# Half of a block's attention by seven half-width products, and the first block's additions ahead of an MLP block's low part

## The chip, the cores and the metric

The kernel runs on one core of one Trainium2 chip. The metric is the device time of one execution in microseconds (us); lower is better. Engines are named as in the profile: PE is TensorE's matmuls, PEld its weight loads, DVE is VectorE, ACT is ScalarE, POOL is GpSimd, SP issues DMAs.

## The reference

`x` is 2048 tokens of 512 features. It is normalised, and an attention branch and an MLP branch are added to it.

```python
def _A_ref(x, wqkv, wo):                      # 32 heads of 16
    q, k, v = split_heads(x @ wqkv)
    phi = lambda t: jnp.where(t > 0, t + 1, jnp.exp(t)) + 1e-6
    pq, pk = phi(q), phi(k)
    kv = jnp.einsum("bhsd,bhse->bhde", pk, v)
    z = jnp.einsum("bhsd->bhd", pk)
    num = jnp.einsum("bhqd,bhde->bhqe", pq, kv)
    den = jnp.einsum("bhqd,bhd->bhq", pq, z)[..., None] + 1e-6
    return join_heads(num / den) @ wo

def _B_ref(x, w1, b1, w2, b2):                # 512 -> 1376 -> 512
    h = jnp.einsum("bsd,df->bsf", x, w1) + b1
    r = jnp.where(h > zero, h, zero)
    return jnp.einsum("bsf,fd->bsd", r * r, w2) + b2

xn = _layernorm(x, axis=-1)
out = x + _A_ref(xn, A_wqkv, A_wo) + _B_ref(xn, B_w1, B_b1, B_w2, B_b2)
```

## The kernel before

The 2048 tokens are 16 tiles of 128, and four tiles are a block of 512 tokens. Every fp32 operand is split into a high part (ScalarE's copy, in a rounded format) and a low part (VectorE's difference, `rest_of` or the second half of `split`), and a product is three matmuls: high by high, high by low, low by high (`PASSES`).

The first stage normalises the tiles and sums keys times tokens. From that one 512 by 512 matrix `m` is made that holds the attention's values and `wo` together, so that the attention's output for a tile is its scaled queries (`aT`) times `m`: four feature chunks of three matmuls, twelve products of 512 columns (`add_attention`).

The second stage runs over two pairs of blocks, `n` = 0 and 1. In a pair, the first-layer products for the two blocks `t1` and `t2` go through a scheme with seven instead of eight products (`product`, in the PSUM banks `b0` to `b3`, tag "ps"). The MLP has 11 feature blocks of 128, the last a ragged one. Its second layer (`mlp_2`, twelve products of 512 columns for four tiles) accumulates in four banks `acc` of the tag "acc"; after `t1` is done, `t2` accumulates in the four banks of the tag "ps" and the roles of the tags change. `wait_for(f)` squares and splits the hidden values of feature block f for `t2`; `waiting` lists these blocks in the order 9, 8, ..., 0, 10. `quarters_2` adds the ragged block's remaining low part by four matmuls of 32 rows each, packed side by side in the array; for `t2` they are the first to write its accumulators.

In the second pair, `t1`'s attention is made by the class `Seven`, also with seven products instead of eight: the block's tokens are halves (rows r), the features are halves (columns c), VectorE makes four sums of `q` in place (`sums_o`) and four of `m` (`sums_m`), both are split into parts (`parts_o`, `parts_m`), and `run` makes one product for one tile of a half as six matmuls of 256 columns. `("a", ...)` names an original quarter of the queries, `("s", ...)` a summed one, `("m", ...)` and `("t", ...)` the same of the matrix. Some products belong to several parts of the result. They go to banks x and y and VectorE adds them from there to the result tiles `res`, which hold `x` and the bias; after that the accumulators are added and each tile is stored. The second block of the pair, `t2`, gets its attention by `add_attention` for all four tiles, after nine of its eleven MLP blocks; the last two MLP blocks (0 and 10) follow tile by tile, with the last tile in two halves (`end`).

The order of instructions on each engine is that of the code. It is written out by hand, partly in tables of counts (`AT`, `AE`) that say how many of the pending small steps (`steps`: phi, the quotients, the splits of `aT`) come at each place. Tiles of one tag rotate through their buffers; an instruction that writes a reused buffer waits for the last reader.

Of the kernel before, what the change touches and what calls it, by code (L numbers as in the profile page):

```python
# [10 lines left out]
OP = mybir.AluOpType  # L11
AX = mybir.AxisListType

P = 128
# [4 lines left out]
def kernel(  # L19
# [30 lines left out]
    nc = tc.nc  # L50
    xf = x.rearrange("b s d -> (b s) d")
    of = out.rearrange("b s d -> (b s) d")
    S, D = xf.shape
    F = w1.shape[1]
    NT = S // P
    NJ = D // P
    TB = 4
    NB = NT // TB
    BT = TB * P
    NF = -(-F // P)  # L60
# [20 lines left out]
    def bank(name, tag="ps"):  # L81
        return psum.tile([P, 512], F32, name=name, tag=tag)
# [54 lines left out]
    def both(name, tags, dt=F32R, pool=keep):  # L137
        return [pool.tile([P, NJ, D], dt, name=f"{name}{u}", tag=t) for u, t in zip("hl", tags)]
# [263 lines left out]
    q = {}  # L402
# [114 lines left out]
    def add_attention(acc, i, last=False):  # L517
        b, k = i // TB, i % TB
        for j in range(NJ):
            a = [aT[b, j][:, u, k * P:(k + 1) * P] for u in range(2)]  # L520
            three(acc[k], a, [m[u][:, j, :] for u in range(2)], False, last and j == NJ - 1)
# [7 lines left out]
    t, rk = two("x0"), four("rk", "r0")  # L529
# [7 lines left out]
    t = two("x2")  # L537
# [17 lines left out]
    for i0 in range(0, NT, TB):  # L555
        a = first_xp[i0]
# [4 lines left out]
        n = TB if i0 >= NPE else TB // 2  # L561
# [36 lines left out]
    for k in range(2):  # L598
        a = slice(k * D // 2, (k + 1) * D // 2)
# [153 lines left out]
    def do(what, k=1):  # L753
        for _ in range(k):
            if what:
                what.pop(0)()
# [57 lines left out]
    for i in range(2, NT):  # L814
# [13 lines left out]
        ps = pks[i] if i < 3 else bank(f"pk{i}")  # L828
# [28 lines left out]
        if i == 12:  # L857
            w = load_1("q", 0)
# [3 lines left out]
        if i == 14:  # L862
            z = pair("w1z0")
# [62 lines left out]
    m = both("m", ("mh", "ml"), pool=work)  # L926
# [43 lines left out]
    LO, HI = slice(0, D // 2), slice(D // 2, D)  # L970

    class Seven:

        def __init__(self, t, acc):
            self.t, self.acc = t, acc
            self.o = [[q[t][:, 2 * c:2 * c + 2, r] for c in range(2)] for r in (LO, HI)]

        def sums_o(self):

# [27 lines left out]

        def parts_o(self):

            self.s = both("so", ("xs1h", "xs1l"))  # L1010
            return self.parts(q[self.t], self.s, ((1, LO), (0, LO), (0, HI), (1, HI)))

        def parts_m(self):

# [2 lines left out]
        def run(self, ps, left, right, e, first=False):  # L1017

            c, r = left[1:]
            for i in range(2):  # L1020
                for n, (u, v) in enumerate(PASSES):
# [4 lines left out]
                    nc.tensor.matmul(ps, lhsT=a, rhs=b, start=first and i == 0 and n == 0, stop=False,  # L1026
                                     skip_group_check=True)


    last = TB - 1  # L1030
    for n in range(2):
        t1, t2 = NB - 1 - 2 * n, NB - 2 - 2 * n
        x1, x2 = xsb
# [24 lines left out]
        steps = {t1: [], t2: []}  # L1058
        r2 = [work.tile([P, k, 512], F32, name=f"r2{u}{n}", tag=f"r{u}") for u, k in zip("abc", (4, 4, 3))]
        waiting = [*range(NF - 2, -1, -1), NF - 1]  # L1060
# [32 lines left out]
        w = load_1(*order[1])  # L1093
        s = {}
# [23 lines left out]


        banks = [bank(f"b{n}_{k}") for k in range(4)]  # L1120
        t5, res, biased = None, {}, []

        def load_res(t):
            for k in range(2):
# [17 lines left out]
        def add(ps, t, k, a=0, z=D):  # L1142
            r = res[t, k]
            nc.vector.tensor_tensor(out=r[:, a:z], in0=ps, in1=r[:, a:z], op=OP.add)  # L1144
# [5 lines left out]
        def step(k=1):  # L1150

            for _ in range(k):
                do(steps[t1] or steps[t2])
# [6 lines left out]
        for p in range(NO + 1):  # L1160
            at_p = AT[p]
            kind, k = order[p] if p < NO else ("", 0)
            fa, fb = 2 * k, 2 * k + 1

            was, k = order[p - 1] if p else ("", 0)
# [27 lines left out]
            if kind:  # L1193
                c11 = w512(f"c11_{n}_{p}", "p", 6)
                copy("act", c11, A)
                product(B, A12, [x[:, 2:] for x in x1], True, True)
                if kind == "w":
                    high_2()
                nc.vector.tensor_tensor(out=c11 if kind == "w" else q[t1][:, fa], in0=B, in1=c11, op=OP.add)
                if kind == "w":  # L1200
                    relu(c11, c11, fa)
                else:
                    steps[t1] += steps_of(t1, fa, parts=True)
                if (n, p) == (0, 0):
                    last_sums(3, difference_high, difference_low)
                if n and p == NO - 1:
                    seven = Seven(t1, acc)
                    sums = seven.sums_o()
                    do(sums, 3)
                step(at_p[0])  # L1210
# [26 lines left out]
            t5 = t5_  # L1237
# [4 lines left out]
            if p == 1:  # L1242
                nc.vector.tensor_scalar(zc[:, 1], zc[:, 0], 1e-6, None, op0=OP.mult)
                acc = [bank(f"acc{t1}_{k}", "acc") for k in range(TB)]
# [92 lines left out]
        def wait_for(f):  # L1337
            name = f"s{n}_{t2}_{f}"
            if f < NF - 1:
                s[f] = hidden_2(name, r2[f])  # L1340
            else:
                s[f], rests = hidden_last(name, r2[f])
                rests()
# [16 lines left out]
        f = NF - 2  # L1360
# [12 lines left out]
        for g in waiting[4:9]:  # L1373
            w2next.extend(piece_2(g, place(g)))
        if n:
            y0, x0, x1_, y1 = (bank(f"seven{k}")[:, LO] for k in range(4))
            xs_, ys_ = (x0, x1_), (y0, y1)
            for e in range(2):
                seven.run(xs_[e], ("a", 0, 0), ("m", 0, LO), e, True)
            for e in range(2):  # L1380
                add(xs_[e], t1, e, 0, D // 2)
            for e in range(2):
                seven.run(acc[e][:, LO], ("a", 1, 0), ("m", 1, LO), e)
            for e in range(2):
                seven.run(acc[e][:, HI], ("s", 1, 0), ("m", 1, HI), e)
            do(lows_m, 4)
            for k in range(TB):
                three(acc[k], [s1[:, u, k * P:(k + 1) * P] for u in range(2)], w2s[f], False, False)
            wait_for(waiting[0])
            for e in range(2):  # L1390
                seven.run(xs_[e], ("s", 0, 0), ("t", 1, HI), e)
            for e in range(2):
                add(xs_[e], t1, 2 + e, 0, D // 2)
            wait_for(waiting[1])
            lqs.append(square_last())
            for e in range(2):
                seven.run(ys_[e], ("s", 0, 1), ("t", 0, HI), e, True)
            for e in range(2):
                seven.run(xs_[e], ("s", 1, 1), ("t", 0, LO), e)
            for e in range(2):  # L1400
                r = res[t1, 2 + e].rearrange("p (a z) -> p a z", a=2)
                nc.vector.tensor_tensor(out=r, in0=ys_[e][:, None, :].to_broadcast([P, 2, D // 2]), in1=r, op=OP.add)
            for e in range(2):
                for k in (e, 2 + e):
                    r = res[t1, k]
                    nc.vector.tensor_tensor(out=r[:, HI], in0=xs_[e], in1=r[:, HI], op=OP.add)
            for e in range(2):
                seven.run(acc[2 + e][:, LO], ("a", 1, 1), ("t", 1, LO), e)
        else:
            add_attention(acc, t1 * TB)  # L1410
            wait_for(waiting[0])
            for k in range(1, TB):
                add_attention(acc, t1 * TB + k)
                if k == 2:
                    wait_for(waiting[1])
                if k == 2:
                    lqs.append(square_last())
# [17 lines left out]
        for e, f in enumerate(waiting[:-2]):  # L1435
            mlp_2(acc, f, s.pop(f))
            if e + 3 < NF - 2:
                wait_for(waiting[e + 3])
            if e:
                do(w2next, 2)  # L1440
                if e + 8 < NF:
                    g = waiting[e + 8]
                    w2next.extend(piece_2(g, place(g)))
            if e == 2:
                load_res(t2)
            if e == 4:
                bias = add_bias()
            if e in ((5, 6) if n else (7, 8)):
                do(bias)
            do(prepare, (1, 0, 0, 1, 0, 2, 2, 3, 1, 3, 1)[e])  # L1450
            if n == 0:
                if e == 3:
                    rawz = raw_1(NF - 1)
                if e == 4:
                    z = pair("w1z1")
                    w = load_1("q", 0)
                if e == 6:
                    columns_high(x2, f2)
                if e == 7:
                    split(z[:, 0], z[:, 1], rawz, "act", "dve")  # L1460
                    columns_high(x1, f1)
            step(AE[e])
            if e and 0 < len(parts_2) and len(steps[t2]) <= 5 * (len(parts_2) - 1):
                do(parts_2)
        do(prepare, len(prepare))
        step(len(steps[t2]))
        do(parts_2, NJ)
        for k in range(TB):
            add_attention(acc, t2 * TB + k, n == 1 and k == last)
            if n == 1 and k < 2:  # L1470
                wait_for(last_two[1 - k])
            if n == 0:
                if k == 0:
                    columns_low(x2, f2)
                    for f in reversed(last_two):
                        wait_for(f)
                    columns_low(x1, f1)
                    prepare = operands_first(1, w)
                if k in (0, 2):
                    do(prepare, 2 if k == 0 else 3)  # L1480
# [43 lines left out]
```

## Time and profile before

| | |
|---|---|
| median of 3 runs | 409.03 us (408.76 to 409.52) |
| the profiled execution | 409.1 us, span 407.4 us |
| TensorE matmul, weight loads busy | 401.8 us (99%), 332.3 us (82%) |
| VectorE, ScalarE busy | 321.4 us (79%), 272.7 us (67%) |
| granted TensorE clock | 1.0 |

The span is what the profiler recorded from the first to the last instruction; the execution's own time has 1.7 us more around it. Matmuls overlap in the rows: a row's duration holds the latency of its last product, so the pace is read from start to start. The stretch that matters lies at the end: `t1`'s attention and last MLP block from 349 to 362 us, `t2`'s MLP blocks from 363.5 to 388 us, its attention from 388 to 399 us, the last two MLP blocks to 404 us, and the last store to 407.4 us.

### The profile page before, as it was taken

What the parts mean: (1) busy time and instruction counts of PE and PEld (TensorE: products, weight loads), DVE (VectorE), ACT (ScalarE), POOL (GpSimd) and SP (SyncE); (2) the same over time, 40 slices, a digit from 0 to 9 for tenths busy, and PEclk for the clock granted to TensorE, in tenths of its full rate; (3) what the DMA queues carried; (4) which work ended last, traced back from release to release, by engine and by line L of the source; (5) the groups of instructions that cost most, each with busy time, mean ns of one, the idle gap of its engine ahead of it and who ended that gap; (6) DMA issues with size and microseconds to landing.
All of it is one profiled execution on the core that took longest, in us unless ns stands there. A gap on an engine that the chain in (4) does not pass through costs nothing.

```text
span 407.4 us, 5755 instructions
## 1 busy us (share of the span) xinstructions
PE 401.8 (99%) x1975; PEld 332.3 (82%) x1975; DVE 321.4 (79%) x585; ACT 272.7 (67%) x474; POOL 49.8 (12%) x81
## 2 busy tenths in 40 slices
PE   8999999999999999999999999999999999999996
PEld 7788888888788888888878888888888888888885
DVE  5886666587898989988349997667989688999833
ACT  5677677556788788886818752667687858947430
POOL 5443333220000000030000300000000200000300
PEclk9999999999999999999999999999999999999999
DMA  6857656910553231381564913321121765025712
GB/s 214 275 169 227 202 165 197 257 27 0 136 177 80 77 103 27 109 200 28 208 232 139 199 25 107 112 53 51 51 80 43 217 116 219 2 79 181 103 26 103
DMA packets 47550, 51.10 MB, mean 125 GB/s; under 512 B 8417, under 2 KB 31201, under 8 KB 47138
## 3 DMA queue, kind: packets, MB, share of 16 engines
q1 hardware_dynamic: 45138, 46.55, 37.2%
q0 software_dynamic: 2304, 4.20, 6.7%
q8 instruction: 15, 0.25, 0.2%
q14 instruction: 13, 0.11, 0.1%
q10 hardware_dynamic: 80, 0.00, 0.0%
HBM read 38.81 MB, written 10.75 MB: 122 GB/s over the span
## 4 chain that ended last, share of the span: by engine, by line
PE 97%; DMA 1%; ACT 0%; SPq 0%; DVE 0%; issue 0%
PE acc L133 35%; PE b L497 33%; PE pk L378 11%; PE kx L398 11%; PE acc L508 2%; PE seven L1026 1%; PE pz L133 1%; DMA rk<-in_A_wqkv_dram 1%; PE acc L1026 1%; PE b L133 1%; PE pz0b L133 1%; PE acc L515 0%; PE pkv L937 0%; PE pm L954 0%; PE pt L310 0%; SPq L161 0%
## 5 line engine op out<-in xcount | busy, mean ns | idle before, releaser
L133 PE MATMUL acc<-w2r,s 128*128 128x512 f32 x477 | 113.1, 390 | 0.0
L133 PEld LDWEIGHTS acc<-w2r,s 128*128 128x128 f32 x477 | 89.3, 188 | 19.1 <-issue 0.6
L497 PE MATMUL b<-T,aop 128*128 128x512 f32 x336 | 83.5, 389 | 0.0
L497 PEld LDWEIGHTS b<-T,aop 128*128 128x128 f32 x336 | 63.0, 188 | 13.9 <-ACT t L114 0.8
L1136 POOL DMA_DIRECT2D res<-in_B_b_dram x16 | 14.4, 1083 | 277.3 <-DMA res<-in_A_x_dram 91.5
L398 PE MATMUL kx<-pk,tok 128*128 128x512 f32 x192 | 46.1, 389 | 0.0
L398 PEld LDWEIGHTS kx<-pk,tok 128*128 128x128 f32 x192 | 36.0, 188 | 7.7 <-ACT pk L114 0.2
L497 PE MATMUL b<-xs0h,aop 128*128 128x512 f32 x112 | 36.9, 390 | 0.0
L114 ACT ACTIVATE aop<-S 128x512 fp32r<-128x512 f32 x28 | 17.5, 625 | 12.6 <-DVE S L735 12.6
L133 PE MATMUL acc<-mh,aTsr 128*128 128x512 f32 x80 | 25.6, 389 | 0.0
L359 POOL TENSOR_TENSOR tok<-xp,tok 128x512 fp32r<-128x512 f32 x15 | 20.2, 1346 | 39.8 <-ACT tok L114 39.8
L497 PEld LDWEIGHTS b<-xs0h,aop 128*128 128x128 f32 x112 | 21.0, 188 | 4.4
L125 DVE TENSOR_TENSOR w2r<-r,w2r 128x512 fp32r<-128x512 f32 (+2 forms) x35 | 23.8, 682 | 0.5 <-ACT w2r L114 0.4
L114 ACT ACTIVATE w2r<-r 128x512 fp32r<-128x512 f32 x32 | 19.7, 621 | 6.7 <-PE acc L133 6.0
L122 DVE TENSOR_TENSOR aop<-S,aop 128x512 fp32r<-128x512 f32 x28 | 19.3, 689 | 4.8 <-ACT aop L114 4.4
L497 PE MATMUL b<-xs0l,aop 128*128 128x512 f32 x56 | 21.8, 389 | 0.0
L1144 DVE TENSOR_TENSOR res<-acc,res 128x512 f32<-128x512 f32 x16 | 10.5, 688 | 14.0 <-PE acc L133 12.7
L122 DVE TENSOR_TENSOR s<-c,s 128x512 fp32r<-128x512 f32 x20 | 13.6, 689 | 8.7 <-ACT s L114 8.6
L497 PE MATMUL b<-xs1h,aop 128*128 128x512 f32 x56 | 19.5, 389 | 0.0
L114 ACT ACTIVATE T<-Tf 128x512 fp32r<-128x512 f32 x16 | 9.5, 625 | 14.4 <-DVE Tf L678 14.3
L114 ACT ACTIVATE c<-b 128x512 f32<-128x512 f32 x28 | 16.4, 587 | 2.5 <-PE b L497 2.4
L133 PEld LDWEIGHTS acc<-mh,aTsr 128*128 128x128 f32 x80 | 15.0, 188 | 3.1
(228 smaller groups left out, 804.7 us busy)
## 6 DMA issues: line engine op xcount, KB each, us to landing
r<-in_B_w_dram SPq DMA_DIRECT2D x49, 256.0 KB, 3.4
res<-in_A_x_dram SPq DMA_DIRECT2D x8, 512.0 KB, 4.7
res<-in_B_b_dram POOLq DMA_DIRECT2D x16, 256.0 KB, 5.9
out_dram<-res SPq DMA_DIRECT2D x15, 256.0 KB, 2.2
via<-xp SPq DMA_DIRECT2D x5, 512.0 KB, 2.6
xg<-via SPq DMA_DIRECT2D x20, 128.0 KB, 2.8
xTd<-t SPq DMA_DIRECT2D x8, 256.0 KB, 3.4
x<-in_A_x_dram SPq DMA_DIRECT2D x4, 512.0 KB, 4.2
```

Of the source, the lines that this page charges most:

```text
L114: nc.scalar.activation(o, i, AF.Copy, bias=bias)
L122: ENG[el].tensor_tensor(out=l, in0=src, in1=f32(h), op=OP.subtract)
L125: nc.vector.tensor_tensor(out=l, in0=src, in1=f32(h), op=OP.subtract)
L133: nc.tensor.matmul(ps, lhsT=a[u], rhs=b[v], start=first and n == 0, stop=last and n == 2)
L359: ENG[el].tensor_tensor(out=l, in0=src, in1=f32(h), op=OP.subtract)
L378: nc.tensor.matmul(ps, lhsT=cols(i)[u][:, j, slot(i)], rhs=w[v][:, j, :], start=first and n == 0, stop=last and n == len(steps) - 1)
L398: nc.tensor.matmul(kxp[c], lhsT=tok[i][:, u, c * P:(c + 1) * P], rhs=pk[i][:, v], start=i == 0 and (u, v) == first, stop=i == NT - 1 and ( ...
L497: nc.tensor.matmul(ps, lhsT=a[u][:, j * P:(j + 1) * P], rhs=b[v][:, j, :], start=first and j == 0 and n == 0, stop=last and j == 1 and n == 2,
L508: nc.tensor.matmul(ps, lhsT=s[u][:, k * P:(k + 1) * P], rhs=w2s[NF - 1][u][:, a:z], start=first and u == 0, stop=stop and u == 1)
L1026: nc.tensor.matmul(ps, lhsT=a, rhs=b, start=first and i == 0 and n == 0, stop=False, skip_group_check=True)
L1136: nc.gpsimd.dma_start(r[:, i], b2[None, :].partition_broadcast(P), accum_op=OP.add)
L1144: nc.vector.tensor_tensor(out=r[:, a:z], in0=ps, in1=r[:, a:z], op=OP.add)
```

## The change

Two things change, both in the second pair.

`Seven` takes a list of tiles of each half, and for `t2` a second object, `half`, covers the first tile of each half: tiles 0 and 2. Its attention is made by seven runs of six 256-column matmuls; tiles 1 and 3 keep `add_attention`. Its sums and parts are made during `t2`'s MLP blocks on 128-token quarters (2 x 128 elements a partition). The matrix's sums are those of `t1`. Two banks, `xh` and `yh`, are taken from the tag "acc".

In `t1`, `wait_for(waiting[1])` (feature block 8) moves from before `square_last` to behind the additions from x and y, and the four banks are taken in the order y0, x0, y1, x1 instead of y0, x0, x1, y1.

```diff
     class Seven:
-        def __init__(self, t, acc):
-            self.t, self.acc = t, acc
-            self.o = [[q[t][:, 2 * c:2 * c + 2, r] for c in range(2)] for r in (LO, HI)]
+        def __init__(self, t, pairs=range(2)):
+            self.t = t
+            self.at = [slice(r * BT // 2 + pairs[0] * P, r * BT // 2 + (pairs[-1] + 1) * P) for r in range(2)]
+            self.o = [[q[t][:, 2 * c:2 * c + 2, at] for c in range(2)] for at in self.at]
...
+        def into(self, ps, k, a):
+            r = res[self.t, k][:, a]
+            if a != LO and a != HI:
+                r, ps = r.rearrange("p (a z) -> p a z", a=2), ps[:, None, :].to_broadcast([P, 2, D // 2])
+            nc.vector.tensor_tensor(out=r, in0=ps, in1=r, op=OP.add)
...
         if n:
-            y0, x0, x1_, y1 = (bank(f"seven{k}")[:, LO] for k in range(4))
-            xs_, ys_ = (x0, x1_), (y0, y1)
+            ys_, xs_ = zip(*((bank(f"y{e}")[:, LO], bank(f"x{e}")[:, LO]) for e in range(2)))
...
-            wait_for(waiting[1])
             lqs.append(square_last())
             for e in range(2):
                 seven.run(ys_[e], ("s", 0, 1), ("t", 0, HI), e, True)
             for e in range(2):
                 seven.run(xs_[e], ("s", 1, 1), ("t", 0, LO), e)
...
             for e in range(2):
                 seven.run(acc[2 + e][:, LO], ("a", 1, 1), ("t", 1, LO), e)
+            wait_for(waiting[1])
...
         for e, f in enumerate(waiting[:-2]):
             mlp_2(acc, f, s.pop(f))
             if e + 3 < NF - 2:
                 wait_for(waiting[e + 3])
+            if n and e == NF - 5:
+                do(highs_o, 4)
+                do(lows_o, 4)
...
             step(AE[e])
+            if n and e == NF - 6:
+                step(len(steps[t2]))
+                half = Seven(t2, (0,))
+                half.mt = seven.mt
+                sums = half.sums_o()
+                highs_o, lows_o = half.parts_o()
...
+            if n and e == NF - 6:
+                do(parts_2, NJ)
+                do(sums, 4)
...
-        for k in range(TB):
-            add_attention(acc, t2 * TB + k, n == 1 and k == last)
-            if n == 1 and k < 2:
-                wait_for(last_two[1 - k])
+        if n:
+            xh, yh = (bank(f"{w}h", "acc")[:, LO] for w in "xy")
+            half.run(xh, ("a", 0, 0), ("m", 0, LO), 0, True)
+            half.run(acc[0][:, LO], ("a", 1, 0), ("m", 1, LO), 0)
+            half.run(acc[2][:, LO], ("a", 1, 1), ("t", 1, LO), 0)
+            half.into(xh, 0, LO)
+            for f in reversed(last_two):
+                wait_for(f)
+            add_attention(acc, t2 * TB + 1)
+            add_attention(acc, t2 * TB + last, True)
+            half.run(acc[0][:, HI], ("s", 1, 0), ("m", 1, HI), 0)
+            half.run(xh, ("s", 0, 0), ("t", 1, HI), 0)
+            half.run(yh, ("s", 0, 1), ("t", 0, HI), 0, True)
+            half.into(xh, 2, LO)
+            half.run(xh, ("s", 1, 1), ("t", 0, LO), 0)
+            half.into(yh, 2, ALL)
+            for k in (0, 2):
+                half.into(xh, k, HI)
+        for k in range(TB) if n == 0 else ():
+            add_attention(acc, t2 * TB + k)
```

Below, the runs of `half` are called by their operands: a00, a10, a11, s10, s00, s01, s11.

The first place is VectorE in `t1`, from the low part of feature block 8 (`s_0_8`) to the last addition from the banks (`seven_3357` is x1, `seven_3355` and `seven_3358` are y0 and y1). Before:

```order
L122 TENSOR_TENSOR s_0_8_3432<-r2a_2493,s_0_8_3432 128x512
L125 TENSOR_TENSOR s1q<-r2c_2495,hq_3436 32x128 x4
L1402 TENSOR_TENSOR res_1_3051<-seven_3355,res_1_3051 128x512
L1402 TENSOR_TENSOR res_1_3051<-seven_3358,res_1_3051 128x512
L1406 TENSOR_TENSOR res_0_3049<-seven_3356,res_0_3049 128x256
L1406 TENSOR_TENSOR res_1_3051<-seven_3356,res_1_3051 128x256
L1406 TENSOR_TENSOR res_0_3049<-seven_3357,res_0_3049 128x256
L1406 TENSOR_TENSOR res_1_3051<-seven_3357,res_1_3051 128x256
```

Now (line numbers here are the changed kernel's; L1036 is `into`):

```order
L125 TENSOR_TENSOR s1q<-r2c_2495,hq_3432 32x128 x4
L1036 TENSOR_TENSOR res_1_3051<-y_3355,res_1_3051 128x512
L1036 TENSOR_TENSOR res_1_3051<-y_3357,res_1_3051 128x512
L1036 TENSOR_TENSOR res_0_3049<-x_3356,res_0_3049 128x256
L1036 TENSOR_TENSOR res_1_3051<-x_3356,res_1_3051 128x256
L1036 TENSOR_TENSOR res_0_3049<-x_3358,res_0_3049 128x256
L1036 TENSOR_TENSOR res_1_3051<-x_3358,res_1_3051 128x256
L122 TENSOR_TENSOR s_0_8_3482<-r2a_2493,s_0_8_3482 128x512
```

The low part of block 8 has moved from the front of these eight to their end; everything else keeps its order.

The second place is VectorE at the end of `t2`, from the last split of `aT` on (`so0h`, `so0l` are the parts of `half`'s sums, `w2r` the last two pieces of w2, `s_0_10` and `s_0_0` the last two MLP blocks). Before:

```order
L122 TENSOR_TENSOR aTsr_3498<-q_2510,aTsr_3498 128x512
L125 TENSOR_TENSOR w2r_1020<-r_0_3554,w2r_1020 128x512
L125 TENSOR_TENSOR w2r_1020<-r_10_3581,w2r_1020 64x512
L125 TENSOR_TENSOR w2r_1020<-r_10_3581,w2r_1020 32x512
L125 TENSOR_TENSOR s_0_10_3731<-r2c_2495,s_0_10_3731 64x512
L122 TENSOR_TENSOR s_0_0_3748<-r2c_2495,s_0_0_3748 128x512
L1144 TENSOR_TENSOR res_1_3587<-acc_3_3488,res_1_3587 128x512
L1144 TENSOR_TENSOR res_0_3585<-acc_0_3485,res_0_3585 128x512
```

Now, up to the same two low parts, and then the additions:

```order
L986 TENSOR_TENSOR q_2510<-q_2510 128x2x128 x4
L125 TENSOR_TENSOR so0l<-q_2510,so0h 128x2x128 x4
L125 TENSOR_TENSOR w2r_1020<-r_0_3554,w2r_1020 128x512
L125 TENSOR_TENSOR w2r_1020<-r_10_3581,w2r_1020 64x512
L125 TENSOR_TENSOR w2r_1020<-r_10_3581,w2r_1020 32x512
L1036 TENSOR_TENSOR res_0_3585<-xh,res_0_3585 128x256
L125 TENSOR_TENSOR s_0_10_3754<-r2c_2495,s_0_10_3754 64x512
L122 TENSOR_TENSOR s_0_0_3759<-r2c_2495,s_0_0_3759 128x512
L1036 TENSOR_TENSOR res_1_3587<-xh,res_1_3587 128x256
L1036 TENSOR_TENSOR res_1_3587<-yh,res_1_3587 128x512
L1036 TENSOR_TENSOR res_0_3585<-xh,res_0_3585 128x256
L1036 TENSOR_TENSOR res_1_3587<-xh,res_1_3587 128x256
```

Eight small instructions stand ahead of the last pieces of w2, and five additions are new, four of them ahead of that of accumulator 3. ScalarE has the four copies to `so0h` at the corresponding place, between its copy to `aTsr` and its copies to `w2r`.

The third place is TensorE where `t2`'s attention begins. Before, tile 0's twelve wide products, of which these are the first half:

```order
L133 MATMUL acc_0_3485<-mh,aTsr_3497 128x512
L133 MATMUL acc_0_3485<-ml,aTsr_3497 128x512
L133 MATMUL acc_0_3485<-mh,aTsr_3497 128x512 x2
L133 MATMUL acc_0_3485<-ml,aTsr_3497 128x512
L133 MATMUL acc_0_3485<-mh,aTsr_3497 128x512
```

Now, the runs a00 and a10 in that place:

```order
L1028 MATMUL xh<-mh,aTsr_3497 128x256
L1028 MATMUL xh<-ml,aTsr_3497 128x256
L1028 MATMUL xh<-mh,aTsr_3497 128x256 x2
L1028 MATMUL xh<-ml,aTsr_3497 128x256
L1028 MATMUL xh<-mh,aTsr_3497 128x256
L1028 MATMUL acc_0_3485<-mh,aTsr_3498 128x256
L1028 MATMUL acc_0_3485<-ml,aTsr_3498 128x256
L1028 MATMUL acc_0_3485<-mh,aTsr_3498 128x256 x2
L1028 MATMUL acc_0_3485<-ml,aTsr_3498 128x256
L1028 MATMUL acc_0_3485<-mh,aTsr_3498 128x256
```

The products are half as wide, and the second feature half (`aTsr_3498`) is reached after six narrow instead of six wide products. The runs s10, s00, s01 and s11 stand behind tiles 1 and 3, right ahead of the last two MLP blocks.

More of the change, by code (lines that the diff above doesn't have):

```diff
@@ L1008, in parts_o @@
         def parts_o(self):
-            self.s = both("so", ("xs1h", "xs1l"))
-            return self.parts(q[self.t], self.s, ((1, LO), (0, LO), (0, HI), (1, HI)))
+            self.s = both(f"so{self.t}", ("xs1h", "xs1l"))
+            one, two = self.at
+            return self.parts(q[self.t], self.s, ((1, one), (0, one), (0, two), (1, two)))
         def parts_m(self):
@@ L1027, in run @@
                                      skip_group_check=True)
+        def into(self, ps, k, a):
[3 more added lines that the diff above has]
+            nc.vector.tensor_tensor(out=r, in0=ps, in1=r, op=OP.add)
+    ALL = slice(0, D)
     last = TB - 1
+    res = {}
     for n in range(2):
@@ L1120 @@
         banks = [bank(f"b{n}_{k}") for k in range(4)]
-        t5, res, biased = None, {}, []
+        t5, biased = None, []
         def load_res(t):
@@ L1206 @@
                 if n and p == NO - 1:
-                    seven = Seven(t1, acc)
+                    seven = Seven(t1)
                     sums = seven.sums_o()
@@ L1380 @@
             for e in range(2):
-                add(xs_[e], t1, e, 0, D // 2)
+                seven.into(xs_[e], e, LO)
             for e in range(2):
@@ L1392 @@
             for e in range(2):
-                add(xs_[e], t1, 2 + e, 0, D // 2)
-            wait_for(waiting[1])
+                seven.into(xs_[e], 2 + e, LO)
             lqs.append(square_last())
@@ L1400 @@
             for e in range(2):
-                r = res[t1, 2 + e].rearrange("p (a z) -> p a z", a=2)
-                nc.vector.tensor_tensor(out=r, in0=ys_[e][:, None, :].to_broadcast([P, 2, D // 2]), in1=r, op=OP.add)
+                seven.into(ys_[e], 2 + e, ALL)
             for e in range(2):
                 for k in (e, 2 + e):
-                    r = res[t1, k]
-                    nc.vector.tensor_tensor(out=r[:, HI], in0=xs_[e], in1=r[:, HI], op=OP.add)
+                    seven.into(xs_[e], k, HI)
             for e in range(2):
                 seven.run(acc[2 + e][:, LO], ("a", 1, 1), ("t", 1, LO), e)
+            wait_for(waiting[1])
         else:
```

## The prediction

> **What bounds the kernel now.** First the page: engines, then the chain that ended last.
>
> ```profile
> PE 401.8 (99%) x1975; PEld 332.3 (82%) x1975; DVE 321.4 (79%) x585; ACT 272.7 (67%) x474; POOL 49.8 (12%) x81
> PE 97%; DMA 1%; ACT 0%; SPq 0%; DVE 0%; issue 0%
> ```
>
> TensorE is busy for 99% of the span and is 97% of the chain. Time goes only if TensorE does less, waits less, or is left waiting by something new. Which waits it has near the change, the view of the weight loads' waits from 340 us on tells, and the timeline gives the price, beside the same place of the first pair (207 us), where nothing waits:
>
> ```profile
> PEld acc L515 <- DVE res L1406: 0.4, 1, 0.4
> ...
> 207.67 0.51 PE L515 MATMUL acc<-w2q,sz0q 32*128 32x512 f32 x4
> 208.34 1.43 PE L133 MATMUL acc<-w2r,s 128*128 128x512 f32 x5
> 362.39 0.51 PE L515 MATMUL acc<-w2q,sz1q 32*128 32x512 f32 x4
> 362.50 0.19 PEld L515 LDWEIGHTS acc<-w2q,s1q 32*128 32x128 f32 x3
> 363.10 0.18 PEld L515 LDWEIGHTS acc<-w2q,s1q 32*128 32x128 f32 x1 [0.41 <-DVE res L1406]
> 363.52 1.23 PEld L133 LDWEIGHTS acc<-w2r,s 128*128 128x128 f32 x6 [0.24 <-issue]
> ```
>
> The eight packed products take 208.34 - 207.67 = 0.67 us where nothing is late, and 363.52 - 362.39 = 1.13 us here. The stall is 0.46 us, and it is the fourth load's, which waits for VectorE to have read a bank (line 1406).
>
> **Term 1: the half by seven products.** The chain in order of time gives the pace of wide and narrow products, the timeline the attention that is replaced:
>
> ```profile
> 281.67 2.72 PE acc L133 x12
> 349.68 1.44 PE seven L1026 x12
> 356.73 4.31 PE seven L1026 x36
> ...
> 388.16 0.39 PE L133 MATMUL acc<-mh,aTsr 128*128 128x512 f32 x1
> 399.05 0.85 PE L133 MATMUL acc<-w2r,s 128*128 128x512 f32 x3
> ```
>
> A 512-column product takes 2.72/12 = 0.2267 us, a 256-column one 1.44/12 = 0.120 (4.31/36 = 0.1197). Twice the narrow one is 0.239, so each product carries a fixed 0.013 us whatever its width. The last block's attention is 48 products in 399.05 - 388.16 = 10.89 us. The change keeps two tiles so (24 products) and makes the other two by seven sums of six narrow products, 42 instead of 24 wide: 24 x 0.2267 = 5.44 us go, 42 x 0.1197 = 5.03 come, and 0.41 us is saved, not the eighth (0.68) that the arithmetic alone would give.
>
> The Trainium skill (TensorE: Matmul & The Clock Gate, Back-to-back issue gap) has N/2.4 + 2.5 ns per product, by which the exchange would save an estimated 24 x 0.2158 - 42 x 0.1092 = 0.59 us and the whole change 0.97. Its sustained figures in the same section, 131 ns at 512 columns and 81 at 128, speak against narrow products altogether. The rows above disagree with both: 227 and 120 ns, each with its own weight load.
>
> **Term 2: the first block's additions.** VectorE ahead of the stall, and the last product of the run that the last additions need:
>
> ```profile
> 358.19 0.43 DVE L1144 TENSOR_TENSOR res<-seven,res 128x256 f32<-128x256 f32 x1 [0.29 <-PE seven L1026]
> 358.54 0.68 DVE L122 TENSOR_TENSOR s<-r2a,s 128x512 fp32r<-128x512 f32 x1
> 359.23 1.17 DVE L125 TENSOR_TENSOR s1q<-r2c,hq 32x128 fp32r<-32x128 f32 x4
> 360.43 1.29 DVE L1402 TENSOR_TENSOR res<-seven,res 128x512 f32<-128x512 f32 x2
> 361.64 1.41 DVE L1406 TENSOR_TENSOR res<-seven,res 128x256 f32<-128x256 f32 x4
> 362.96 2.48 DVE L1144 TENSOR_TENSOR res<-acc,res 128x512 f32<-128x512 f32 x4
> ...
> 360.75 0.28 PE L1026 MATMUL seven<-mth,sol 128*128 128x256 f32 x1
> ```
>
> The 358.54 row is the low part of MLP block 8; it now stands behind the four additions. What was behind it comes 359.23 - 358.54 = 0.69 us earlier: the last addition ends at 361.64 + 1.41 - 0.69 = 362.36 instead of 363.05. Nothing on TensorE holds it up: the x1 run ends at 360.75 + 0.28 = 361.03, and x1's additions would start near 361.6. Loads two to four of the packed products went at 362.50, so the fourth finds its bank read with some 0.1 us to spare, and the whole 0.46 us goes. The moved low part then runs at 362.3 to 363.0 and is needed by the second MLP block's third product, 0.46 us earlier than now: 363.52 - 0.46 + 2.72 + 0.45 = 366.2. The accumulators' additions (362.96 row) wait for the packed products anyway, so VectorE's order from 363 us on keeps its times. ScalarE only swaps two pairs (the ragged last feature block's square and copy before block 8's) and has results 2 us ahead; no DMA is moved here.
>
> What is late next? TensorE reaches each following MLP block 0.46 us sooner while VectorE stays. The tightest operand is the low part of w2 for block 2:
>
> ```profile
> 381.11 0.68 DVE L125 TENSOR_TENSOR w2r<-r,w2r 128x512 fp32r<-128x512 f32 x1
> ```
>
> It ends at 381.79. Seven blocks of twelve after 363.06, the second product of the eighth is due at 363.06 + 85 x 0.2267 = 382.33. The margin is 0.5 us, so no new wait.
>
> **Term 3: what the half adds beside TensorE.** VectorE's and ScalarE's end, and the nearest rows for 256-element work:
>
> ```profile
> 387.64 0.69 DVE L122 TENSOR_TENSOR aTsr<-q,aTsr 128x512 fp32r<-128x512 f32 x1 [0.70 <-ACT aTsr L114]
> 391.00 0.69 DVE L122 TENSOR_TENSOR s<-r2c,s 128x512 fp32r<-128x512 f32 x1
> 399.25 0.69 DVE L1144 TENSOR_TENSOR res<-acc,res 128x512 f32<-128x512 f32 x1 [7.56 <-PE acc L133]
> 400.39 0.69 DVE L1144 TENSOR_TENSOR res<-acc,res 128x512 f32<-128x512 f32 x1 [0.44 <-PE acc L508]
> 403.85 0.42 DVE L1144 TENSOR_TENSOR res<-end,res 128x256 f32<-128x256 f32 x1 [0.17 <-PE end L508]
> 387.52 1.14 ACT L114 ACTIVATE w2r<-r 128x512 fp32r<-128x512 f32 x2
> 389.73 0.64 ACT L114 ACTIVATE s<-r2c 128x512 fp32r<-128x512 f32 x1
> ...
> L735 DVE TENSOR_TENSOR S<-S,r 128x256 f32<-128x256 f32 x10 | 4.3, 425 | 0.3
> L114 ACT ACTIVATE aop<-r 128x256 fp32r<-128x256 f32 x10 | 4.1, 407 | 0.0
> ```
>
> Behind the last attention split (ends 388.33) come four sums, four ScalarE copies, four low parts, all on 2 x 128 elements, a shape the trace does not show. Bounds are a 128x256 row (0.42) and a full 128x512 row (0.69); I take 0.42, the same count of elements. The sums depend on each other: 388.3 + 4 x 0.46 = 390.1. Copies follow to 391.4 and low parts to 392.0. ScalarE's last five instructions, 390.37 - 387.52 = 2.85 us now, then end at 394.2, the last low part (block 0) at about 395.5 with the first xh addition before it. Due times: attention's tiles start at 388.16 - 0.46 = 387.70; 18 narrow (2.16) and 24 wide products (5.44) come first, so the sums' parts are due at 395.3, the last MLP blocks at 398.3. The cover is 3 us. At 0.69 a piece the low parts end near 394.5 and still fit. The two DMAs that now sit behind the later ScalarE copies have as much room. POOL's queue is untouched.
>
> One new wait has no cover: the bank xh is read (`into`, left half of the third tile's result) after the s00 run and written again by the s11 run, with only one run of six (0.72 us) between. From the timeline, a run's last product and the addition that waits for it:
>
> ```profile
> 357.15 0.28 PE L1026 MATMUL seven<-mth,sol 128*128 128x256 f32 x1
> 357.48 0.42 DVE L1144 TENSOR_TENSOR res<-seven,res 128x256 f32<-128x256 f32 x1 [0.41 <-PE seven L1026]
> ```
>
> From the last product's start to the addition's end is 357.48 + 0.42 - 357.15 = 0.75 us, and the wait's end to the load about 0.05 (363.05 to 363.10 above). So the load goes 0.80 us after that start; undisturbed it would go at 6 x 0.12 = 0.72. Cost 0.08 us, bounds 0 and 0.2 (the exposed load's 0.1 on top).
>
> At the end VectorE has four additions more. The first of x and the one of y fall beside the s01 and s11 runs. After s11 come two of x and that of accumulator 3, about 1.3 us, while TensorE's first tile of the last MLP blocks takes 400.39 - 399.25 = 1.14 us and VectorE was idle 0.44 us of it. It is behind by 0.2 us at tile 0 and level at tile 1. The tail from the last addition (403.85 + 0.42 = 404.27) to the span's end at 407.4 keeps its 3.1 us.
>
> **The sum.** -0.46 - 0.41 + 0.08 = -0.79 us (from -0.67 to -0.87). The profiled execution took 409.1 us (span 407.4), 0.07 over the median 409.03; from the median the forecast is 408.24, rounded 408.2.
>
> **Rivals.**
>
> - *The stall stays or moves (chance 0.10).* The fourth load has only 0.1 us to spare. For: the order of the four banks was also changed, and one slow addition uses up the margin. Against: 0.69 us is removed against a stall of 0.46. Keeping all of it gives -0.33 us, 408.7.
> - *VectorE becomes the bound of the end, slower (0.08).* The chain sum, copy, low part, w2 parts, last MLP parts runs through two engines in order, and TensorE's s10 and s11 runs stand behind it. It decides when block 0's low part ends past 396.9 us, where the xh addition behind it is due: 1.4 us later than worked out. Each us beyond that is a us; 2.2 us late altogether cancels the gain, 3.2 us gives about 410.0. For: 2 x 128 operands and the handovers are unmeasured. Against: at 0.69 for each it is still in time.
> - *The change does more than I count* (inside the forecast): no cost at xh, -0.87 us, 408.16.
>
> **How the numbers follow.** 0.2% (0.82 us) is about what a measurement of this kernel can tell from no change; the three runs shown lie from 0.27 below to 0.49 above their median. My 0.79 us stands almost on that line. The forecast (0.82) is therefore split: 0.49 beyond it, 0.33 within. The first rival adds 0.09 within and 0.01 beyond, the second is slower. That makes 0.50, 0.42 and 0.08. The range runs from 408.2 less 0.4 (run spread and no xh cost) to 408.7 plus 0.2 for the first rival.
>
> **What would show it.** Right: the four s1q loads together near 362.5 and line 133 at 363.06; attention from its first product to the last MLP pair in 10.55 us; VectorE idle before the xh additions. Wrong: a weight-load wait over 0.2 us anywhere after 349 us, narrow products slower than 0.12 us, or VectorE busy without a gap up to 397 us.

## The result

| | before | changed |
|---|---|---|
| median of 21 runs | 408.96 us (408.76 to 409.52) | 408.14 us (407.89 to 409.68) |
| ratio to before | | 0.9982, 95% interval 0.9975 to 0.9988 |
| the profiled execution, its span | 409.1 us, 407.4 us | 408.15 us, 406.4 us |

The ratio is 0.74 us less (0.49 to 1.02); the forecast was 0.79 us less than 409.03, or 408.24. Beside other kernels on another chip the same kernel gave 0.9988 (0.9980 to 0.9997), 408.39 us of 409.0.

The page of the changed kernel, engines and the chain's engines:

```profile
PE 401.5 (99%) x1993; PEld 333.1 (82%) x1993; DVE 326.7 (80%) x598; ACT 274.0 (67%) x478; POOL 49.7 (12%) x81
PE 97%; DMA 1%; DVE 1%; ACT 0%; issue 0%
```

TensorE bounds it as before, with 18 products more. The spans differ by 1.0 us, more than the change gives: 0.15 us of it lies ahead of the change, where the kernels are alike (the first block's attention begins at 349.36 instead of 349.51 us). Two profiles of the changed kernel alone reach the first packed product at 362.24 and 362.60 us. So all stages below are measured from the first packed product (sz1q, near 362 us) to the end of VectorE's last addition. That is 403.85 + 0.42 - 362.39 = 41.88 us before.

The first block's packed products and VectorE ahead of them, in the changed kernel's timeline (L1036 is `into`):

```profile
358.50 1.17 DVE L125 TENSOR_TENSOR s1q<-r2c,hq 32x128 fp32r<-32x128 f32 x4
359.70 1.29 DVE L1036 TENSOR_TENSOR res<-y,res 128x512 f32<-128x512 f32 x2
360.91 1.40 DVE L1036 TENSOR_TENSOR res<-x,res 128x256 f32<-128x256 f32 x4
362.23 0.68 DVE L122 TENSOR_TENSOR s<-r2a,s 128x512 fp32r<-128x512 f32 x1
362.24 0.51 PE L515 MATMUL acc<-w2q,sz1q 32*128 32x512 f32 x4
362.34 0.20 PEld L515 LDWEIGHTS acc<-w2q,s1q 32*128 32x128 f32 x4
362.91 0.95 PE L133 MATMUL acc<-w2r,s 128*128 128x512 f32 x3
```

The last addition ends at 362.31, all four s1q loads go together at 362.34, and line 133 follows 362.91 - 362.24 = 0.67 us after the first packed product, where it was 1.13. The stall is gone, and with only 0.03 us between the addition's end and the loads.

The last block's attention in the same timeline: TensorE's products, two of its weight loads around the start of s11, and then VectorE:

```profile
387.50 0.28 PE L1028 MATMUL xh<-mh,aTsr 128*128 128x256 f32 x1
389.65 0.39 PE L133 MATMUL acc<-mh,aTsr 128*128 128x512 f32 x1
395.11 0.29 PE L1028 MATMUL acc<-mh,so0h 128*128 128x256 f32 x1
396.44 0.28 PE L1028 MATMUL xh<-mth,so0l 128*128 128x256 f32 x1
397.15 0.28 PE L1028 MATMUL yh<-mth,so0l 128*128 128x256 f32 x1
397.33 0.36 PE L1028 MATMUL xh<-mth,so0h 128*128 128x256 f32 x1
397.52 0.28 PE L1028 MATMUL xh<-mtl,so0h 128*128 128x256 f32 x1
398.11 0.86 PE L133 MATMUL acc<-w2r,s 128*128 128x512 f32 x3
...
397.04 0.19 PEld L1028 LDWEIGHTS yh<-mth,so0l 128*128 128x128 f32 x1
397.30 0.19 PEld L1028 LDWEIGHTS xh<-mth,so0h 128*128 128x128 f32 x1
...
388.27 1.80 DVE L986 TENSOR_TENSOR q<-q 128x256 f32<-128x256 f32 x4
390.55 1.43 DVE L125 TENSOR_TENSOR so0l<-q,so0h 128x256 fp32r<-128x256 f32 x4 [0.48 <-ACT so0h L114]
394.04 0.42 DVE L1036 TENSOR_TENSOR res<-xh,res 128x256 f32<-128x256 f32 x1
395.21 0.69 DVE L122 TENSOR_TENSOR s<-r2c,s 128x512 fp32r<-128x512 f32 x1
396.76 0.42 DVE L1036 TENSOR_TENSOR res<-xh,res 128x256 f32<-128x256 f32 x1 [0.86 <-PE xh L1028]
398.31 0.76 DVE L1036 TENSOR_TENSOR res<-xh,res 128x256 f32<-128x256 f32 x2 [0.15 <-PE xh L1028]
398.99 1.28 DVE L1155 TENSOR_TENSOR res<-acc,res 128x512 f32<-128x512 f32 x2
400.61 0.69 DVE L1155 TENSOR_TENSOR res<-acc,res 128x512 f32<-128x512 f32 x1 [0.35 <-PE acc L508]
402.93 0.42 DVE L1155 TENSOR_TENSOR res<-end,res 128x256 f32<-128x256 f32 x1 [0.17 <-PE end L508]
```

The attention is 398.11 - 387.50 = 10.61 us, 0.28 less than the 10.89 before. The 18 narrow products take 2.15 us and the two plain tiles 5.46; the other 24 narrow ones take 3.00 instead of 2.87, and the missing 0.13 stands at the beginning of the run s11 (397.15 to 397.33 to 397.52, where 0.12 is the pace). The first load of s11 went at 397.30, 0.26 us after the load ahead of it, and 0.12 us after VectorE had read the bank (396.76 + 0.42 = 397.18). VectorE has 0.86 us to spare before the xh addition. The stage ends at 402.93 + 0.42 = 403.35, 41.11 us after the first packed product: 0.77 less than before.

### The profile page after: what moved, and what is told of

Same layout as the page of the kernel before. It is cut to its first block, busy times and chain, and to the rows that moved or that the text cites. A ratio compares the mean times of both kernels' runs of the same rounds, so it can differ in the third digit from the quotient of the medians.

```text
span 406.4 us, 5813 instructions
## 1 busy us (share of the span) xinstructions
PE 401.5 (99%) x1993; PEld 333.1 (82%) x1993; DVE 326.7 (80%) x598; ACT 274.0 (67%) x478; POOL 49.7 (12%) x81
## 4 chain that ended last, share of the span: by engine, by line
PE 97%; DMA 1%; DVE 1%; ACT 0%; issue 0%
PE acc L133 33%; PE b L497 33%; PE pk L378 11%; PE kx L398 11%; PE acc L508 2%; PE acc L1028 2%; PE pz L133 1%; PE x L1028 1%; DMA x<-in_A_x_dram 1%; PE b L133 1%; PE pz0b L133 1%; PE xh L1028 1%; PE y L1028 0%; PE acc L515 0%; PE pt L310 0%; DVE st L236 0%
## 5 line engine op out<-in xcount | busy, mean ns | idle before, releaser
L133 PE MATMUL acc<-mh,aTsr 128*128 128x512 f32 x64 | 20.7, 389 | 0.0
L369 ACT ACTIVATE k<-pk 128x512 f32<-128x512 f32 x16 | 9.4, 590 | 9.9 <-PE pk L378 9.8
L114 ACT ACTIVATE pk<-k 128x512 fp32r<-128x512 f32 x16 | 10.1, 631 | 8.6 <-DVE k L373 8.5
```

The costliest lines, as they stand in the source:

```text
L114: nc.scalar.activation(o, i, AF.Copy, bias=bias)
L133: nc.tensor.matmul(ps, lhsT=a[u], rhs=b[v], start=first and n == 0, stop=last and n == 2)
L369: nc.scalar.activation(p, ps, AF.Relu, scale=-1.0)
```

## Experiments

Stage lengths are taken as above from each kernel's profile; two profiles of one kernel agree within 0.01 us in them where the granted clock is 1.00, while whole times need 0.3 us or more to be told apart.

**The two parts alone.** First, the kernel before with only this edit:

```diff
-            wait_for(waiting[1])
             lqs.append(square_last())
...
                 seven.run(acc[2 + e][:, LO], ("a", 1, 1), ("t", 1, LO), e)
+            wait_for(waiting[1])
```

> The kernel before with one edit: block 8's wait_for stands behind the first block's additions; the banks keep their order and the half keeps its wide products. Theory (the two parts are separate terms): 0.46 us less, the fourth s1q load goes with the other three, line 133 starts 0.67 us after the packed products begin. Rival (the bank order is needed too, the stall stays or moves to the third load): within 0.15 us of before.

408.42 us, ratio 0.9985 (0.9976 to 0.9993), 0.61 us less (0.29 to 0.98). Its timeline:

```profile
362.36 0.51 PE L515 MATMUL acc<-w2q,sz1q 32*128 32x512 f32 x4
362.70 0.41 PE L515 MATMUL acc<-w2q,s1q 32*128 32x512 f32 x4
363.04 1.18 PE L133 MATMUL acc<-w2r,s 128*128 128x512 f32 x4
...
403.31 0.42 DVE L1144 TENSOR_TENSOR res<-end,res 128x256 f32<-128x256 f32 x1 [0.17 <-PE end L508]
```

0.68 us for the packed products; the stage is 41.37 us, 0.51 less. The move alone removes the stall, without the new bank order. Second, only the bank order:

```diff
-            y0, x0, x1_, y1 = (bank(f"seven{k}")[:, LO] for k in range(4))
-            xs_, ys_ = (x0, x1_), (y0, y1)
+            ys_, xs_ = zip(*((bank(f"y{e}")[:, LO], bank(f"x{e}")[:, LO]) for e in range(2)))
```

> The kernel before with only the new order of the four banks (y0, x0, y1, x1). Theory (the last x addition sets the stall, whichever bank holds x1): the fourth load waits as before, same time within 0.1 us. Rival (the order alone lets the loads go): up to 0.46 us less.

408.85 us, ratio 0.9993 (0.9982 to 1.0004). The weight loads' waits in its profile:

```profile
PEld acc L515 <- DVE res L1405: 0.4, 1, 0.4
```

And its timeline:

```profile
362.09 0.51 PE L515 MATMUL acc<-w2q,sz1q 32*128 32x512 f32 x4
362.81 0.18 PEld L515 LDWEIGHTS acc<-w2q,s1q 32*128 32x128 f32 x1 [0.42 <-DVE res L1405]
363.24 0.97 PE L133 MATMUL acc<-w2r,s 128*128 128x512 f32 x3
```

The wait is there as before (1.15 us for the packed products, stage 41.89). The order of the banks does nothing by itself. Third, the half alone: the changed kernel with the first block's old order and place.

> The changed kernel with the first block as before (old place of block 8's low part, old bank order); only the half by seven products is new. Theory: 42 narrow for 24 wide products give 0.41 us, the wait at xh costs 0.13 us as in the trace of after, so 0.28 us less than before, with the 0.46 us stall at line 515 still there. Rival (the half gains nothing, all of the change's gain is the stall's): within 0.1 us of before.

```profile
362.48 0.51 PE L515 MATMUL acc<-w2q,sz1q 32*128 32x512 f32 x4
363.62 0.72 PE L133 MATMUL acc<-w2r,s 128*128 128x512 f32 x2
388.21 0.28 PE L1028 MATMUL xh<-mh,aTsr 128*128 128x256 f32 x1
398.82 0.86 PE L133 MATMUL acc<-w2r,s 128*128 128x512 f32 x3
403.64 0.42 DVE L1155 TENSOR_TENSOR res<-end,res 128x256 f32<-128x256 f32 x1 [0.17 <-PE end L508]
```

In this timeline the stall is back (1.14 us), the attention takes 10.61 us, and the stage is 41.58 us, 0.30 less than before. The time doesn't resolve it: 408.87 us, 0.9999 (0.9990 to 1.0007), where the theory says 0.9993. It was run again beside the changed kernel:

> The half alone once more, because the first interval held both answers. Theory: 0.28 us less than before. Rival: 0.0 us.

408.80 us, 0.9997 (0.9989 to 1.0006), stage 41.57. The interval still holds both answers; only the trace tells that the half is worth 0.30 us. The parts' 0.51 and 0.30 add up to 0.81, the whole gives 0.77. Each of the three holds some 0.05 us of the MLP blocks between the two places: from line 133's first product to the attention's first they take 24.59 us instead of 24.64 (363.52 to 388.16), so the sum counts this twice. No run shows what it comes from.

**The price of a narrow product.** The kernel before, with tiles 0 and 2 as plain products of half width, two passes over the columns:

```diff
-            add_attention(acc, t2 * TB + k, n == 1 and k == last)
+            if n and k in (0, 2):
+                for z in (LO, HI):
+                    for j in range(NJ):
+                        a = [aT[t2, j][:, u, k * P:(k + 1) * P] for u in range(2)]
+                        three(acc[k][:, z], a, [x[:, j, z] for x in m], False, False)
+            else:
+                add_attention(acc, t2 * TB + k, n == 1 and k == last)
```

> The kernel before, where tiles 0 and 2 of the last block's attention are made as 48 plain products of 256 columns instead of 24 of 512; no sums, no additions. This measures the cost of a narrow product by itself. Theory (a product costs 0.013 us beside its columns): 48 x 0.1197 - 24 x 0.2267 = 0.31 us more than before. Rival (narrow products are exactly half as dear as wide ones): same as before. Rival (they have a floor of their own, 131 ns or more): 0.85 us more or beyond.

409.46 us, ratio 1.0019 (1.0008 to 1.0029), 0.78 us more (0.33 to 1.19). Two of its eleven executions, 410.74 and 411.16 us, lift that; the medians are 0.48 us apart. Its attention in the timeline:

```profile
388.40 0.28 PE L133 MATMUL acc<-mh,aTsr 128*128 128x256 f32 x1
399.65 0.85 PE L133 MATMUL acc<-w2r,s 128*128 128x512 f32 x3
```

11.25 us, 0.36 more than the 10.89 with wide products. The same arithmetic in narrow products costs 0.36/24 = 0.015 us for each product added, near the 0.013 of the prediction. So of the eighth that the seven products save (0.68 us), this takes 0.27, xh 0.13, and 0.28 is left.

**The wait at xh.** The changed kernel with the run s10 moved between s01 and s11:

```diff
-            half.run(acc[0][:, HI], ("s", 1, 0), ("m", 1, HI), 0)
             half.run(xh, ("s", 0, 0), ("t", 1, HI), 0)
             half.run(yh, ("s", 0, 1), ("t", 0, HI), 0, True)
             half.into(xh, 2, LO)
+            half.run(acc[0][:, HI], ("s", 1, 0), ("m", 1, HI), 0)
             half.run(xh, ("s", 1, 1), ("t", 0, LO), 0)
```

> The changed kernel with the runs of the half in the order s00, s01, s10, s11, so that two runs stand between xh's reading and its next writing. Theory (the 0.13 us at xh is VectorE's reading of the bank between s00 and s11): s11 starts 0.12 us after the run ahead of it, 0.13 us less than the changed kernel, 0.95 us less than before. Rival (the gap is the change of operands or of bank, not VectorE): the gap stays, same time as the changed kernel.

408.15 us, ratio 0.9981 (0.9972 to 0.9990). The timeline: the attention's first product, then s10's last, s11's first and the first of the last two MLP blocks:

```profile
387.85 0.28 PE L1028 MATMUL xh<-mh,aTsr 128*128 128x256 f32 x1
397.49 0.28 PE L1028 MATMUL acc<-mh,so0l 128*128 128x256 f32 x1
397.61 0.28 PE L1028 MATMUL xh<-mth,so0h 128*128 128x256 f32 x1
398.32 0.86 PE L133 MATMUL acc<-w2r,s 128*128 128x512 f32 x3
```

The gap is gone: 0.12 us from product to product, the attention 10.47 us, the stage 40.97, 0.14 less than the changed kernel. The operands and banks of s11 are the same as there, so it was VectorE's reading. Both kernels were then run on one chip:

> The changed kernel itself, beside the next two on one chip. Theory: 0.75 us less than before, and in the trace 0.13 us between the s01 and s11 runs more than their pace.

> The reordered runs once more, beside the changed kernel. Theory: the wait at xh is real time, so 0.13 us less than the changed kernel, 0.2% under before. Rival (the end is given back elsewhere, as VectorE is behind at tile 0): the same as the changed kernel.

The changed kernel 408.39 us (0.9988, 0.9980 to 0.9997; stage 41.12), the reordered one 408.07 us (0.9976, 0.9966 to 0.9986; stage 40.97). These times point the way of the trace, but the intervals overlap, and the first ratio of the reordered kernel, 0.9981, was practically the changed kernel's 0.9982 in the result. So the 0.14 us rests on the traces. It is the quickest of the kernels here, 0.98 us under before (0.57 to 1.39).

**The cover.** What hides the half's sums, copies and low parts are tiles 1 and 3. The changed kernel with those two lines behind the seven runs:

```diff
-            add_attention(acc, t2 * TB + 1)
-            add_attention(acc, t2 * TB + last, True)
...
             half.run(xh, ("s", 1, 1), ("t", 0, LO), 0)
+            add_attention(acc, t2 * TB + 1)
+            add_attention(acc, t2 * TB + last, True)
```

> The changed kernel with the plain tiles 1 and 3 moved behind the seven runs; the same products and additions, only without their cover. Theory: s10 waits for the parts until about 391 us, s00 until VectorE has read xh behind the last pieces of w2 near 394.5 us, s11 until the last MLP parts are made, near 396.7 us; about 4.8 us more than the changed kernel. Rival (VectorE would reorder nothing but is early enough): under 1 us more.

414.16 us, ratio 1.0130 (1.0114 to 1.0145), 5.3 us more than before. TensorE's waits in its profile (us in total, times, longest):

```profile
PE xh L1028 <- DVE res L1036: 2.8, 1, 2.8
PE acc L1028 <- ACT so0h L114: 0.7, 1, 0.7
```

Two of its windows (length, busy time of PE, PEld, DVE, ACT and POOL, then the granted clock, DMA share and GB/s):

```profile
392.00:394.00 2.00, 0.02 (x1) 0.00 (x0) 1.96 (x4) 1.97 (x5) 0.00 (x0) 1.00 0.05 13
396.00:398.00 2.00, 2.00 (x11) 2.00 (x11) 1.16 (x3) 0.00 (x0) 0.00 (x0) 0.50 0.00 0
```

Two narrow products from its timeline, one after the other:

```profile
396.19 0.41 PE L1028 MATMUL yh<-mth,so0h 128*128 128x256 f32 x1
396.40 0.42 PE L1028 MATMUL yh<-mtl,so0h 128*128 128x256 f32 x1
```

Two of the three expected waits came, for the parts and for xh behind w2's last pieces. The third, of s11 until near 396.7 us, does not show: s11 began at 396.83 anyway. For from 395.7 us on, about 1 us after the wait of 2.8 us, the products took 0.21 us instead of 0.12, at a granted clock of 0.50 that lasted 3.4 us. The theory's 4.8 us over the changed kernel was 5.7 by the stages (46.77 to 41.11). The slow products took about 1.5 us more than at their pace (an estimate from the rows of this stretch), which is more than the difference.

All four tiles by seven products, without plain tiles between:

```diff
-                half = Seven(t2, (0,))
+                half = Seven(t2)
...
+            for e in range(2):
+                half.run(xs_[e], ("a", 0, 0), ("m", 0, LO), e, True)
```

and so on for both pairs, in four banks xh0, xh1, yh0, yh1. (The flag that ends the accumulation is set elsewhere too, as no plain tile is left to set it.)

> The changed kernel with all four tiles of the last block by seven products, so that no plain tile stands between the runs on original quarters and those on sums. Theory (the half works because tiles 1 and 3 cover VectorE and ScalarE): another 0.41 us of products goes, but s00 waits until VectorE has read the x banks behind w2's last pieces, near 396.5 us; about 2.7 us more than the changed kernel, 1.9 us more than before. Rival (the sums and parts are hidden anyway): about 0.3 us less than the changed kernel.

412.73 us, ratio 1.0087 (1.0059 to 1.0116). The profiled execution took 411.05 us with a span of 409.3. Its stage is 44.20 us, 3.1 more than the changed kernel, where 2.7 was expected, with the clock at 1.00 from 388 us to the end. The wait in its timeline:

```profile
393.54 0.28 PE L1028 MATMUL acc<-mh,so0l 128*128 128x256 f32 x1
396.64 0.36 PE L1028 MATMUL xh<-mth,so0h 128*128 128x256 f32 x1 [2.82 <-DVE res L1036]
```

Of its other executions one took 411.64 us and two 413.8 to 413.9. The kernel was run once more:

> All four tiles by seven products once more: two of four executions took 2.5 us more than the other two. Theory (the 3 us wait of TensorE lets its granted clock drop in some executions, as in the trace without cover): a slow execution shows a stretch at 0.5 clock after the wait, a quick one does not. Rival (VectorE or a DMA is late in the slow ones): the clock stays at 1.0 and a wait is longer.

412.68 and 413.28 us; the profiled one was the first, with a span of 411.0. Its waits are the same, and its windows read:

```profile
396.00:398.00 2.00, 1.25 (x10) 1.28 (x11) 1.91 (x5) 0.01 (x1) 0.00 (x0) 0.98 0.32 71
398.00:400.00 2.00, 2.00 (x11) 2.00 (x10) 1.14 (x3) 0.00 (x0) 0.00 (x0) 0.50 0.00 0
400.00:402.00 2.00, 2.00 (x13) 2.00 (x13) 1.38 (x2) 0.00 (x0) 0.00 (x0) 0.66 0.04 8
402.00:404.00 2.00, 2.00 (x13) 1.76 (x12) 1.85 (x5) 0.00 (x0) 0.00 (x0) 1.00 0.00 0
```

The clock was at half for about 3.4 us, and the stage is 45.74 us, 1.5 us longer than in the other profile (the spans differ by 1.7). The same wait of 2.8 us was followed by the half clock in this execution and not in the other. The two at 413.8 us have no trace, but the mean granted clock of each execution was recorded: 0.992 in these two, 0.996 in the one whose windows stand above, 0.999 in the two quick ones. Their spans are 2.8 us longer than that of the first profile (412.1 to 409.3), nearly twice what the half clock cost above, at twice the loss of clock. So the clock would account for them too, though no trace shows where they lost it.

## Why the prediction was right

- *Term 2, the stall*: 0.46 us forecast, 0.46 measured (1.13 to 0.67), and it goes by the move alone (0.45 in that kernel). The margin was smaller than worked out: VectorE's last addition ended 0.03 us ahead of the loads, not 0.1, and 0.02 to 0.03 in each of the eight profiles with the move. Where the fourth load had waited, it went 0.05 us after that end, so there is nothing to spare. The first rival stood nearer than its chance of 0.10 says, but in every one of these profiles the four loads went together.
- *Term 1, the half*: -0.41 + 0.08 forecast, -0.28 measured. The products cost what the rows of before gave (0.1197 and 0.2267 us); the mis-sized term is the wait at xh, 0.13 instead of 0.08, inside its bounds of 0 and 0.2. The addition ended 0.74 us after s00's last product had started (396.44 to 397.18), where 0.75 was reckoned; but the load followed 0.12 us behind it, not the 0.05 taken from line 515 (0.74 + 0.12 - 0.72 = 0.14). It does so in every profile where a load waits for xh (0.11 to 0.12 us). Why line 515's wait ends sooner, no run shows.
- *What is late next*: nothing that costs time. The only wait that the view of the weight loads shows is 0.4 us at line 133, right behind the packed products, put to "issue" (0.2 before). By the letter it is the sign of being wrong, a load's wait over 0.2 us, but line 133's product follows 0.67 us after the first packed one all the same. The wait at xh is too short for that view.
- *Term 3, the cover*: the low parts ended at 391.98 (392.0 forecast), block 0's low part at 395.90 instead of 395.5, and 0.86 us of VectorE's idle time was left before xh. Taking the cover away costs 5.7 us of the stage, about 1.5 of them by the half clock, and making the half a whole 3.1: the slower rival's mechanism is real and lay 0.86 us away, not the 1.4 forecast.
- *The end*: VectorE was behind at tile 0 and nearly level at tile 1 (idle 0.35, then 0.44 us), as forecast. The stage is 0.77 us shorter, where the sum had 0.79. That this is so near is in part luck: the 0.05 us by which xh cost more was made up by the 0.05 us of the MLP blocks, which was not forecast. And 0.74 us by the ratio lies as close to the line of 0.82 as the forecast did; on which side of it a measurement falls is no test of the working, the stages are.

## What to carry over

Where one engine is busy for 99% of the span, look for the few places where it waits for a buffer to be read: moving an instruction that isn't due for 3 us behind the readers gave more here than the better arithmetic. Price an algebraic saving by start-to-start times of the shape it will have: of one eighth of two tiles' products, two fifths went to the narrower product and a fifth to a bank that was reused too soon. Work made for such a scheme needs other products between its making and its use; the two tiles that were left plain are what makes the half pay.

## What the hardware showed unexpectedly

A wait of TensorE of 2.8 us near the end, in kernels that otherwise run at a granted clock of 1.00, was followed in two of the three profiles that had it by 0.50 for 3.4 us, beginning about 1 us after the products had started again, and then by 1.00. By the mean clocks, 8 of the 10 executions of these two kernels had 0.996 or less; of the 181 others whose clock was recorded 2 had 0.996, one of the kernel before (411.27 us) and one with narrow products (411.16 us). So this wait makes the half clock likely, but it is neither always followed by it nor its only occasion. The Trainium skill (TensorE: Matmul & The Clock Gate, Part 1) has the clock fall to half after an idle window of about 3.4 us that runs freely, and its table under "Why this matters for your kernels" asks for no gap over about 3 us. The half clock, the free phase (one execution had it, one hadn't, at the same wait) and the 3.4 us agree with it; the gap does not, as 2.8 us was enough.

At half clock a narrow product started every 0.214 us, not at twice 0.1197. So such a wait cost either its own length or, with one stretch of half clock, 1.5 us more, and two profiles of one kernel differ by that.
